# Attention and two dense layers on one core: the first loads regrouped, two transfers at the head of ScalarE's queue, attention jobs due sooner

## The chip, the cores and the metric

The kernel runs on one NeuronCore of one Trainium2 chip. The metric is the device time of one execution in microseconds (us), and the number compared is the median of several runs. The five engines are named here as the profile names them: PE is TensorE, DVE is VectorE, ACT is ScalarE, POOL is GpSimd and SP is SyncE, which here only issues transfers.

## The reference

Causal attention over a window with four sink positions feeds two dense layers. All of it is float32.

```python
batch, n_heads, seq, head_dim = (2, 8, 768, 64)
n_sink, window = (4, 128)
scores = scale * np.matmul(q, k.transpose(0, 1, 3, 2))
keep = is_sink | in_window            # in_window: 0 <= row - column < window
scores = np.where(keep, scores, -1000000000.0)
a = np.exp(scores - max); a = a / (sum(a) + 1e-09)
x = (a @ v) as (1536 tokens, 512)
...
h = x @ w_in                          # layer 0: (512, 2048)
g = np.maximum(h, 0.0) + alpha * np.minimum(h, 0.0)
x = g @ w_out
...
h = x @ w_in; r = np.maximum(h, 0.0)  # layer 1
out = (r * r) @ w_out
```

## The kernel before, in words

**Units of work.** Queries are cut into 12 chunks of 128 rows (six for each batch), and the eight heads into two groups of four, so the attention is 24 *jobs*, counted here from 0; job i is group i % 2 of the chunk that stands i // 2-th in `ORDER`. A job is: scores on TensorE into the bank `s` (L515); a masked minimum on VectorE for each of four heads (L528, into `sp` and `nm`); the exponentials on ScalarE (L532); the normalisation by `rc` (L548 on VectorE or L547 on ScalarE); four transposes on TensorE into `t` (L557); a copy to `pc` on either engine (L240); two selections on GpSimd (L571); the sums with the values into `o` (L590); and two rows that write the attention's output `X` as a high part and a remainder (L240, L247). Jobs 0 to 3 belong to first chunks, have no earlier chunk to look at, and are smaller.

The dense layers split each operand into a high part and a remainder, and make a product of three matmuls. The weights come in 512 KB blocks, a *half* for each of 16 slices of the hidden size and each of the two matrices (L276), stand packed as 64-bit values, and have to be unpacked into `w` by ScalarE and VectorE (L280 to L292: `cs`, `x`, high part, remainder). L308 makes h from `X` and `w`, L318 to L328 make `g` from it, and L340 makes the layer's output from `g` and `w`.

**What sets the order.** Each step is given to a planner (`Plan.add`) with a due time, what it reads and writes, and the engines that could do it at an assumed cost. `Plan.issue` then writes the program: it takes again and again the step with the earliest due time among those that could start soon. The planner's costs (`AFTER`, `MORE`, the start values in L680) set the order and the choice of engine, and nothing else. On the chip each engine runs its own list in order, and waits at each instruction for semaphores.

The due times stand in tables. `JOBS` holds those of the 24 jobs, `RAW_LOADS` those of the first 16 weight halves' transfers, `VALUE_LOADS` those of the first two value tiles. All transfers are issued by SP, but for half of the last store. Queries and keys come in one transfer for each job (L495, L496): 128 KB of queries and 160 KB of keys, the keys into one of four places of a tile for each head group. The queries of jobs 0 to 3 lie in `g7`, a tile that the dense layer uses later.

**Semaphores of transfers.** The framework gives every transfer one of eight completion semaphores in turn, DMAHW0 to DMAHW7, in the order in which the program was written, whatever queue issues it. A transfer whose semaphore was used before waits, on the engine that issues it, until the earlier transfer with that semaphore has landed.

Until the first dense matmul, 34 matmuls of an identity (L699, `WARM`) stand between the attention's, to keep TensorE busy.

Of the kernel before, what the change touches and what calls it, by code (L numbers as in the profile page):

```python
# [18 lines left out]
P = 128  # L19
NS = 32  # L20
KC = P + NS
W3 = 2 * P + NS
# [5 lines left out]
AFTER = {"pe": 197, "act": 150, "dve": 128, "pool": 140, "dma": 950}  # L28
MORE = {"pe": 90, "pool": 40, "dma": 1250}
# [20 lines left out]
SOON = -1000.0  # L50
# [4 lines left out]
ORDER = (0, 6, 1, 7, 2, 3, 4, 5, 8, 9, 10, 11)  # L55
# [115 lines left out]
def attn_moe_moe(ctx, tc, q, k, v, vsink, par, alpha, w1, w2, out):  # L171
    nc = tc.nc
    B, NCH, NG, _, QW = q.shape
# [24 lines left out]
    pari = const.tile([P, 4], I32, name="pari")  # L198
# [53 lines left out]
    class Feed:  # L252
# [9 lines left out]
        def half(self, due, layer, f, slot, a, need):  # L262
            add, new = self.plan.add, self.places.new
            wk = f"w{slot}_{a}"
            w = self.w[layer, f, a] = new(wk)
            q = self.halves
            self.halves += 1
            r, more = self.raws(q)
            early = RAW_LOADS[q:q + 1] if self.early else ()
            rk, ck, xk = f"raw{r}", f"cs{q % 2}", f"x{q % 2}"  # L270
            cs, x = new(ck), new(xk)
# [3 lines left out]
            at = due - PARTS + a  # L275
            add(early[0] if early else due - LOAD + a, more, [rk], ("dma", 1456, lambda: nc.sync.dma_start(out=raw(), in_=src)))  # L276
# [122 lines left out]
    class Short:  # L399
# [65 lines left out]
        def start(self):  # L465
            self.K = [self.con.tile([P, 2, 4 * KC], F32, name=f"K{g}") for g in range(NG)]
            self.v, self.sums, self.early = {}, {}, self.places.new("g7")
            for i in range(B * NCH * NG):
                self.job(i, *divmod(ORDER[i // NG], NCH), i % NG)

        def load(self, due, key, get, src, cost):
            self.add(due, [], [key], ("dma", cost, lambda: nc.sync.dma_start(out=get(), in_=src)))

        def values(self, due, at, key, src):
            t = self.places.new(key)
            self.load(due, key, t, src, 728)
            self.v[at] = t, key

        def job(self, i, b, c, g):
            add, new, K = self.add, self.places.new, self.K[g]  # L480
# [6 lines left out]

            if i < 4:

                qk, qt = ("g", 7, i // 2, i % 2 * 2), lambda: self.early()[:, i // 2, i % 2 * 256:i % 2 * 256 + 256].bitcast(  # L490
                    F32).rearrange("p (a s) -> p a s", a=2)
            else:
                qk, qt = ring("q", 2)
            when = JOB_LOADS[i] if i < 4 else due - 8
            self.load(when, qk, qt, q[b, c, g].rearrange("p (a s) -> p a s", a=2), 364)  # L495
            self.load(when, ("K", g, here), lambda: K[:, :, here * KC:(here + 1) * KC],  # L496
                      k[b, c, g].rearrange("p (a s) -> p a s", a=2), 455)
# [103 lines left out]
    def full_attention():  # L601
        with ExitStack() as ctx:
# [22 lines left out]
            for c in range(NCH):  # L625
# [9 lines left out]
                for b in range(B):  # L635
                    for h in range(2 * 4):
# [3 lines left out]
                        nc.sync.dma_start(out=qt, in_=q[b, c, g].rearrange("p (a s) -> p a s", a=2)[rows, pr % 2])  # L640
                        kt = raw.tile([D, S], F32, tag="kt", name="kt")
                        vv = raw.tile([P, NCH, 2 * D], F32, tag="vv", name="vv")
                        for cc in range(NCH):
                            nc.sync.dma_start(out=kt[:, cc * P:(cc + 1) * P],
                                              in_=k[b, cc, g].rearrange("p (a s) -> p a s", a=2)[rows, pr % 2, 0:P])
                            nc.sync.dma_start(out=vv[:, cc], in_=v[b, cc * P:(cc + 1) * P, pr * 2 * D:(pr + 1) * 2 * D])
# [32 lines left out]
    with tc.manual_schedule():  # L679
        plan = Plan({"pe": 2500, "dve": 4500, "pool": 1500, "act": 1300, "dma": 2900})  # L680
# [9 lines left out]
        nc.sync.dma_start(out=pari, in_=par.bitcast(I32).rearrange("(o n) -> o n", o=1).to_broadcast([P, 4]))  # L690
# [157 lines left out]
```

## Time and profile before

| | us |
|---|---|
| median of three runs | 633.65 (633.64 to 634.35) |
| the profiled execution's own time | 635.78 |
| its span, first to last instruction | 634.1 |
| TensorE busy | 618.5 |
| VectorE busy | 390.3 |
| ScalarE busy | 248.5 |

The span is what the profiler shows; the time has 1.7 us around it. The profiled execution is 2.1 us longer than the median of the runs, so a sum made in the trace is a difference that is then taken off the median. Busy time is the time in which an engine had an instruction in work. It overlaps at instruction boundaries (a row that is 0.69 us long may be followed after 0.61 us), so where durations are added up below, the distance from one start to the next is taken.

### The profile page before, as it was taken

What the parts mean: (1) busy time and instruction counts of PE and PEld (TensorE: products, weight loads), DVE (VectorE), ACT (ScalarE), POOL (GpSimd) and SP (SyncE); (2) the same over time, 40 slices, a digit from 0 to 9 for tenths busy, and PEclk for the clock granted to TensorE, in tenths of its full rate; (3) what the DMA queues carried; (4) which work ended last, traced back from release to release, by engine and by line L of the source; (5) the groups of instructions that cost most, each with busy time, mean ns of one, the idle gap of its engine ahead of it and who ended that gap; (6) DMA issues with size and microseconds to landing.
All of it is one profiled execution on the core that took longest, in us unless ns stands there. A gap on an engine that the chain in (4) does not pass through costs nothing.

```text
span 634.1 us, 9086 instructions
## 1 busy us (share of the span) xinstructions
PE 618.5 (98%) x3448; PEld 512.4 (81%) x3448; DVE 390.3 (62%) x927; ACT 248.5 (39%) x579; POOL 29.1 (5%) x48
## 2 busy tenths in 40 slices
PE   8898999999999999999999999999999999999996
PEld 7787877888888888888888788888888888888885
DVE  6899976678846949363389984233496324444342
ACT  4899865545445625120146661210362211010110
POOL 0013122212000000000000000000000000000000
PEclk9799999999999999999999999999999999999999
DMA  7955223210452434100015540000040000101002
GB/s 243 346 181 175 74 84 95 70 44 11 126 174 70 154 101 163 45 1 1 0 33 188 179 133 1 1 0 1 0 133 1 1 0 1 68 0 37 30 1 71
DMA packets 23428, 48.13 MB, mean 76 GB/s; under 512 B 2512, under 2 KB 11984, under 8 KB 23376
## 3 DMA queue, kind: packets, MB, share of 16 engines
q1 hardware_dynamic: 23232, 47.34, 23.2%
q8 instruction: 29, 0.48, 0.3%
q14 instruction: 23, 0.19, 0.1%
q10 hardware_dynamic: 144, 0.13, 0.1%
HBM read 44.31 MB, written 3.15 MB: 75 GB/s over the span
## 4 chain that ended last, share of the span: by engine, by line
PE 80%; DVE 13%; DMA 3%; issue 1%; SPq 1%; ACT 1%; DVEq 0%; ACTq 0%
PE h L308 35%; PE yb L340 28%; PE h L340 10%; PE o L590 4%; PE s L515 3%; DVE w L247 2%; DVE x L289 2%; DMA al<-alpha 2%; DVE r L320 1%; DVE x L286 1%; PE t L557 1%; DVE g L247 1%; DVE sp L528 1%; DMA raw<-w 1%; DVE X L247 1%
## 5 line engine op out<-in xcount | busy, mean ns | idle before, releaser
L308 PE MATMUL h<-X,w 128*128 128x512 f32 (+1 forms) x1248 | 275.9, 375 | 0.3 <-DVE r L320 0.3
L308 PEld LDWEIGHTS h<-X,w 128*128 128x128 f32 x1248 | 222.3, 189 | 42.8 <-DVE r L320 0.7
L340 PE MATMUL yb<-w,g 128*128 128x512 f32 x576 | 134.5, 389 | 0.0
L340 PEld LDWEIGHTS yb<-w,g 128*128 128x128 f32 x576 | 108.1, 188 | 22.4
L325 DVE TENSOR_TENSOR r<-r 128x512 f32<-128x512 f32 x48 | 33.2, 691 | 122.8 <-ACT r L323 122.8
L323 ACT ACTIVATE r<-h 128x512 f32<-128x512 f32 x48 | 28.7, 598 | 174.5 <-PE h L308 174.4
L340 PE MATMUL h<-g,w 128*128 128x512 f32 x288 | 69.5, 395 | 0.1
L247 DVE TENSOR_TENSOR g<-r,g 128x512 fp32r<-128x512 f32 (+1 forms) x104 | 68.2, 657 | 2.2
L340 PE MATMUL yb<-g,w 128*128 128x512 f32 x288 | 68.7, 391 | 0.2 <-DVE g L247 0.2
L340 PEld LDWEIGHTS yb<-g,w 128*128 128x128 f32 x288 | 53.7, 188 | 12.7 <-DVE g L247 1.6
L340 PEld LDWEIGHTS h<-g,w 128*128 128x128 f32 x288 | 53.2, 189 | 11.4 <-ACT Y L240 0.6
L320 DVE SCALAR_TENSOR_TENSOR r<-r,oma,h 128x512 f32<-128x512 f32 (+1 forms) x56 | 37.2, 666 | 36.3 <-ACT r L318 36.3
L318 ACT ACTIVATE r<-h 128x512 f32<-128x512 f32 (+1 forms) x56 | 29.8, 533 | 59.7 <-PE h L308 59.3
L280 ACT ACTIVATE cs<-raw 128x512 f32<-128x512 f32 x56 | 37.6, 675 | 33.2 <-DVE x L289 24.5
L289 DVE SCALAR_TENSOR_TENSOR x<-cs,x 128x512 uint32<-128x512 uint32 x64 | 43.9, 690 | 1.9 <-ACT x L282 0.2
L247 DVE TENSOR_TENSOR w<-x,w 128x512 fp32r<-128x512 f32 x64 | 43.9, 687 | 1.4 <-ACT w L240 0.4
L532 ACT ACTIVATE sp<-sp,nm 128x160 f32<-128x160 f32 (+1 forms) x96 | 39.8, 417 | 9.8 <-DVE nm L528 9.6
L240 DVE CAST g<-r 128x512 fp32r<-128x512 f32 (+1 forms) x69 | 29.1, 422 | 2.8
L240 DVE CAST w<-x 128x512 fp32r<-128x512 f32 x25 | 10.6, 425 | 28.8 <-PE h L308 18.6
L240 ACT CAST w<-x 128x512 fp32r<-128x512 f32 x39 | 24.0, 616 | 7.1 <-DVE x L289 6.4
L515 PE MATMUL s<-K,q 64*128 64x160 f32 (+1 forms) x320 | 26.2, 305 | 0.1
L286 DVE TENSOR_SCALAR x<-raw 128x512 uint16<-128x512 uint16 x56 | 25.5, 460 | 1.0 <-DMA raw<-w 0.8
(84 smaller groups left out, 460.6 us busy)
## 6 DMA issues: line engine op xcount, KB each, us to landing
raw<-w SPq DMA_DIRECT2D x56, 512.0 KB, 3.8
Y<-w SPq DMA_DIRECT2D x8, 512.0 KB, 7.4
K<-k SPq DMA_DIRECT2D x24, 160.0 KB, 3.1
v<-v SPq DMA_DIRECT2D x12, 256.0 KB, 3.8
out<-Y SPq DMA_DIRECT2D x11, 256.0 KB, 2.0
q<-q SPq DMA_DIRECT2D x20, 128.0 KB, 2.3
g<-q SPq DMA_DIRECT2D x4, 128.0 KB, 3.4
vs<-vsink SPq DMA_DIRECT2D x2, 256.0 KB, 5.3
```

Source lines behind the costliest of these rows:

```text
L240: return lambda: f(**dict(zip(("out", "in_"), get())))
L247: nc.vector.tensor_tensor(out=lo, in0=src, in1=hi.bitcast(F32), op=ALU.subtract)
L280: add(at, [rk], [ck], ("act", 560, lambda: nc.scalar.activation(out=cs(), in_=raw()[:, :, 1].bitcast(F32), func=AF.Abs, scale=2.0 ** -112)))
L286: add(at, [rk], [(xk, 0)], ("dve", dve_ns(512, True), lambda: nc.vector.tensor_scalar(half(U16, 0), raw().bitcast(U16).rearrange("p j (w a ...
L289: add(at, [ck, *two(xk)], two(xk), ("dve", dve_ns(512), lambda: nc.vector.scalar_tensor_tensor(out=x(), in0=cs().bitcast(U32), scalar=3, i ...
L308: nc.tensor.matmul(like(h()[:, 0:n], xs), lhsT=wi()[:, a, kt * P:(kt + 1) * P], rhs=xs, start=kt == 0 and i == 0, stop=kt == KT - 1 and i ...
L318: add(SOON + due, [hk], [rk], ("act", act_ns(n, True), lambda: nc.scalar.activation(out=rs(), in_=hs(), func=AF.Relu, scale=-1.0)))
L320: add(SOON + due, [hk, rk, "oma"], [rk], ("dve", dve_ns(n + 60), lambda: nc.vector.scalar_tensor_tensor(out=rs(), in0=rs(), scalar=oma[:, ...
L325: add(SOON + due, [rk], [rk], ("dve", dve_ns(n), lambda: nc.vector.tensor_tensor(out=rs(), in0=rs(), in1=rs(), op=ALU.mult)))
L340: nc.tensor.matmul(y(), lhsT=lhsT, rhs=rhs, start=first and i == 0, stop=last and i == 2)
L515: nc.tensor.matmul(s()[:, 2 * p + j, x:y], lhsT=qt()[rows, p], rhs=K[rows, p, k0:k0 + y - x], start=True, stop=True)
L532: ("act", act_ns(n) + 190, lambda h=h: nc.scalar.activation(out=sp()[:, h, 0:n], in_=sp()[:, h, 0:n], func=AF.Exp, scale=-1.0, bias=nm()[: ...
```

## The change

Queries and keys of a chunk now lie together in memory for all eight heads. Keys come in one transfer of 320 KB for a chunk, into one of four tiles `K0` to `K3`; the queries of jobs 0 and 1, and of jobs 2 and 3, in one of 256 KB each. Later queries still come one job at a time, now due 10 before the job and not 8. The first chunk's queries and keys are issued ahead of the masks, the keys on ScalarE's queue. ScalarE also issues the keys of the second chunk and the first two weight halves. The due times of jobs 4 to 23 are smaller, and the planner's numbers for transfers differ.

```diff
-AFTER = {"pe": 197, "act": 150, "dve": 128, "pool": 140, "dma": 950}
-MORE = {"pe": 90, "pool": 40, "dma": 1250}
+AFTER = {"pe": 197, "act": 150, "dve": 128, "pool": 140, "dma": 2500}
+MORE = {"pe": 90, "pool": 40, "dma": -300}
...
-JOBS = (0, 0.5, 1, 1.5, 10, 14, 18, 22) + tuple(range(38, 118, 5))
+JOBS = (0, 0, 1, 1.5, 8, 8, 11.5, 15.5) + tuple(range(30, 94, 4))
...
-JOB_LOADS = (-10, -10, -9, -8.5)
-VALUE_LOADS = {0: -8, 6: -6.5}
-RAW_LOADS = tuple(-9.5 + 1.5 * x for x in range(16))
+AHEAD = 10
+VALUE_LOADS = {0: -8.8, 6: -7}
+RAW_LOADS = tuple(-8.9 + 1.5 * x for x in range(16))
...
+            by = nc.scalar if early and q < 2 else nc.sync
+            add(early[0] if early else due - LOAD + a, more, [rk], ("dma", 1456, lambda: by.dma_start(out=raw(), in_=src)))
...
+            self.K = [con.tile([P, NG, 2, KC], F32, name=f"K{i}") for i in range(4)]
+            self.early = self.places.new("g7")
+
+            self.queries(0)
+            self.keys(0, 0, nc.scalar)
...
+        def queries(self, i):
+
+            nc.sync.dma_start(out=self.early()[:, i].bitcast(F32).rearrange("p (g n) -> p g n", g=NG),
+                              in_=q[divmod(ORDER[i], NCH)])
+
+        def keys(self, i, place, by):
+            by.dma_start(out=self.K[place].rearrange("p g a n -> p g (a n)"), in_=k[divmod(ORDER[i], NCH)])
...
+                add(due - AHEAD, [], [("K", here)], ("dma", 862, lambda: i and self.keys(
+                    i // NG, here, nc.scalar if i < 4 else nc.sync)))
...
-        plan = Plan({"pe": 2500, "dve": 4500, "pool": 1500, "act": 1300, "dma": 2900})
+        plan = Plan({"pe": 2500, "dve": 4500, "pool": 1500, "act": 2100, "dma": 800})
```

In the changed kernel the lines are numbered anew: 276 is 277, 308 is 309, 340 is 341, and from 515 on the numbers are 14 higher.

**The head of ScalarE's list.** Before, ScalarE (ACT) loads its table, makes one small exponential, and then runs job 0's exponentials. The names in brackets are the semaphores that a row waits for.

```order
L434 ACT_TABLE_LOAD
L434 ACTIVATE flag_60<-ident_90 1x1 [waits Pool_49]
L532 ACTIVATE sp0_150,sm0_155<-sp0_150,nm0_151 128x128 [waits DVE_49] x4
L280 ACTIVATE cs0_183<-raw0_137 128x512 [waits DMAHW5_49]
L532 ACTIVATE sp1_185,sm1_194<-sp1_185,nm1_186 128x128 [waits DVE_49] x4
```

Now (`g7` is the queries' tile, `raw0` and `raw1` hold weight halves):

```order
L483 DMA K0_89<-k 128x640
L441 ACT_TABLE_LOAD
L441 ACTIVATE flag_60<-ident_97 1x1 [waits Pool_49]
L483 DMA K1_90<-k 128x640 [waits DMAHW3_49]
L277 DMA raw0_131<-w1 128x1024 [waits DMAHW5_49]
L277 DMA raw1_150<-w1 128x1024 [waits DMAHW7_49]
L546 ACTIVATE sp0_154,sm0_158<-sp0_154,nm0_155 128x128 [waits DVE_49] x4
L281 ACTIVATE cs0_185<-raw0_131 128x512 [waits DMAHW5_49]
L546 ACTIVATE sp1_187,sm1_195<-sp1_187,nm1_188 128x128 [waits DVE_49] x4
```

Four transfers stand ahead of job 0's exponentials, and three of them wait. By the turn of the eight semaphores, DMAHW3 is that of the second query transfer, DMAHW5 that of `v1` and DMAHW7 that of the first half that goes into `Y0`.

**The head of SP's list.** Before:

```order
L690 DMA pari_63<-par 128x4
L472 DMA g7_118<-q 128x256
L472 DMA K0_114<-k 128x2x160
L472 DMA g7_118<-q 128x256
L472 DMA K1_115<-k 128x2x160
L276 DMA raw0_137<-w1 128x1024
L472 DMA g7_118<-q 128x256
L472 DMA K0_114<-k 128x2x160
L472 DMA g7_118<-q 128x256 [waits DMAHW0_49]
L472 DMA K1_115<-k 128x2x160 [waits DMAHW1_49]
L472 DMA v0_175<-v 128x512 [waits DMAHW2_49]
L276 DMA raw1_181<-w1 128x1024 [waits DMAHW3_49]
```

Now:

```order
L479 DMA g7_93<-q 128x512
L426 DMA pari_63<-par 128x4
L479 DMA g7_93<-q 128x512
L486 DMA v0_148<-v 128x512
L486 DMA v1_169<-v 128x512
L277 DMA raw2_183<-w1 128x1024
L277 DMA Y0_65<-w1 128x1024
L277 DMA Y0_65<-w1 128x1024 [waits DMAHW0_49]
L486 DMA q0_263<-q 128x256 [waits DMAHW1_49]
L483 DMA K2_91<-k 128x640 [waits DMAHW2_49]
L486 DMA q1_284<-q 128x256 [waits DMAHW4_49]
L277 DMA Y0_65<-w1 128x1024 [waits DMAHW6_49]
```

SP's first seven rows now wait for nothing; `raw0`, `raw1` and two key transfers are gone from here, `raw2` and the blocks for `Y0` stand sooner, and `q0`, `K2`, `q1`, which jobs 4 and 5 need, come before the third block for `Y0`.

**TensorE's list around the first dense matmuls.** Before, from job 3's transposes (`s` is a job's scores, `t` its transposes, `o` its sums, `h` a dense product):

```order
L557 MATMUL t_367<-ident_90,sp1_296 128x128 x4
L590 MATMUL o_379<-pc0_359,v1_211 64x128 x4
L515 MATMUL s_390<-K0_114,q0_372 128x160 x2
...
L590 MATMUL o_406<-pc1_382,v1_211 64x128 x4
L308 MATMUL h0_416<-X_64,w0_0_214 128x256 x6
L308 MATMUL h1_429<-X_64,w1_0_290 128x256 x6
...
L308 MATMUL h0_481<-X_64,w2_0_365 128x256 x9
L515 MATMUL s_497<-K1_115,q1_464 128x160 x2
...
L557 MATMUL t_531<-ident_90,sp0_425 128x128 x4
L308 MATMUL h1_538<-X_64,w3_0_409 128x256 x12
L308 MATMUL h0_570<-X_64,w4_0_470 128x256 x12
L590 MATMUL o_520<-ss0_526,vs0_452 64x128 x2
```

Now, from job 4's scores on:

```order
L529 MATMUL s_333<-K0_89,q0_263 128x160 x2
...
L571 MATMUL t_380<-ident_97,sp1_304 128x128 x4
L604 MATMUL o_392<-pc0_363,v1_169 64x128 x4
L529 MATMUL s_400<-K0_89,q1_284 128x160 x2
...
L604 MATMUL o_421<-pc1_395,v1_169 64x128 x4
L309 MATMUL h0_431<-X_64,w0_0_223 128x256 x6
...
L529 MATMUL s_472<-K1_90,q0_355 128x160 x2
...
L571 MATMUL t_492<-ident_97,sp0_366 128x128 x4
L309 MATMUL h1_446<-X_64,w1_0_302 128x256 x6
L309 MATMUL h0_518<-X_64,w2_0_429 128x256 x12
L571 MATMUL t_552<-ident_97,sp1_443 128x128 x4
L604 MATMUL o_489<-ss0_501,vs0_418 64x128 x2
```

Job 4's scores now stand ahead of job 2's transposes, and job 5's ahead of all dense matmuls (before: behind 33 of them); dense matmuls stand behind what were later jobs' rows. Jobs 4, 5, 6 and 7 finish their sums behind 36, 36, 48 and 72 dense matmuls, where it was 60, 84, 96 and 108; by job 10's sums both lists have 204, and from job 12 on the counts differ by 3 at most.

## Rows read from the trace of the kernel before

**Rows 1.** The page: busy us of each engine, then tenths in 40 slices.
```profile
PE 618.5 (98%) x3448; PEld 512.4 (81%) x3448; DVE 390.3 (62%) x927; ACT 248.5 (39%) x579; POOL 29.1 (5%) x48
...
DVE  6899976678846949363389984233496324444342
ACT  4899865545445625120146661210362211010110
```

**Rows 2.** By stretch: length, busy us (x instructions), granted clock, DMA share, GB/s.
```profile
0.00:12.00 12.00, 9.28 (x59) 8.26 (x59) 7.42 (x40) 5.35 (x19) 1.14 (x8) 1.00 0.75 221
12.00:28.00 16.00, 14.10 (x109) 11.44 (x108) 12.97 (x46) 12.50 (x37) 0.00 (x0) 0.82 0.94 336
28.00:88.00 60.00, 55.18 (x544) 48.76 (x545) 59.45 (x195) 53.24 (x159) 11.40 (x14) 0.99 0.50 153
88.00:165.00 77.00, 76.88 (x704) 62.02 (x703) 53.63 (x195) 38.23 (x136) 16.57 (x26) 1.00 0.17 49
```

**Rows 3.** What TensorE waited for from 27 to 130 us: total, times, longest.
```profile
PE o L563 <- DVE X L247: 1.3, 1, 1.3
PE t L557 <- DVE sp L548: 1.3, 1, 1.3
PE o L563 <- DVE mask L542: 1.0, 2, 0.6
```

**Rows 4.** Timeline of ScalarE and VectorE at the start; idle before in brackets.
```profile
7.19 0.40 ACT L532 ACTIVATE sp<-sp,nm 128x128 f32<-128x128 f32 x1 [4.89 <-DVE nm L528]
...
8.37 0.47 DVE L284 TENSOR_SCALAR x<-raw 128x512 uint16<-128x512 uint16 x1 [0.59 <-DMA raw<-w]
...
13.65 0.69 ACT L280 ACTIVATE cs<-raw 128x512 f32<-128x512 f32 x1 [2.26 <-DMA raw<-w]
```

**Rows 5.** Transfers, first 40 us: GB/s by us; KB, us to landing.
```profile
GB/s 0 0 53 254 197 256 290 353 326 261 299 369 283 231 330 410 414 434 406 391 374 411 407 383 131 213 213 342 335 308 406 376 394 123 49 197 321 187 327 293
...
raw<-w SPq DMA_DIRECT2D x6, 512.0 KB, 7.1
K<-k SPq DMA_DIRECT2D x10, 160.0 KB, 4.5
v<-v SPq DMA_DIRECT2D x4, 256.0 KB, 5.2
```

**Rows 6.** Transfers issued from 1.0 to 1.5 us: KB each, us to landing.
```profile
g<-q SPq DMA_DIRECT2D x1, 128.0 KB, 2.6
```

**Rows 7.** Timeline of VectorE from 28.5 to 69 us, rows that follow each other.
```profile
28.50 0.42 DVE L247 TENSOR_TENSOR X<-o,X 128x256 fp32r<-128x256 f32 x1
28.84 0.31 DVE L528 CUSTOM_DVE_ANT_0 sp<-s,mask 128x160 f32<-128x160 f32 x1
...
29.56 0.69 DVE L247 TENSOR_TENSOR w<-x,w 128x512 fp32r<-128x512 f32 x1
30.17 0.68 DVE L289 SCALAR_TENSOR_TENSOR x<-cs,x 128x512 uint32<-128x512 uint32 x1
30.77 0.16 DVE L537 TENSOR_SCALAR rc<-sm 128x4 f32<-128x4 f32 x1
30.84 0.46 DVE L284 TENSOR_SCALAR x<-Y 128x512 uint16<-128x512 uint16 x1
31.19 0.47 DVE L320 SCALAR_TENSOR_TENSOR r<-r,oma,h 128x256 f32<-128x256 f32 x1
...
68.58 0.69 DVE L548 TENSOR_TENSOR sp<-sp,rc 128x512 f32<-128x512 f32 x1
```

**Rows 8.** Timeline of TensorE at four places.
```profile
24.53 2.29 PE L515 MATMUL s<-K,q 64*128 64x160 f32 x16
...
27.80 3.63 PE L308 MATMUL h<-X,w 128*128 128x256 f32 x24
...
64.77 1.26 PE L515 MATMUL s<-K,q 64*128 64x160 f32 x16
...
69.42 0.62 PE L557 MATMUL t<-ident,sp 128*128 128x128 f32 x4
```

More of the change, by code (lines that the diff above doesn't have):

```diff
@@ L419, in masks @@
             con = self.con
+            self.K = [con.tile([P, NG, 2, KC], F32, name=f"K{i}") for i in range(4)]
+            self.early = self.places.new("g7")
+            self.queries(0)
+            self.keys(0, 0, nc.scalar)
+            nc.sync.dma_start(out=pari, in_=par.bitcast(I32).rearrange("(o n) -> o n", o=1).to_broadcast([P, 4]))
             self.ident = con.tile([P, P], F32, name="ident")
@@ L465, in start, with load @@
         def start(self):
-            self.K = [self.con.tile([P, 2, 4 * KC], F32, name=f"K{g}") for g in range(NG)]
-            self.v, self.sums, self.early = {}, {}, self.places.new("g7")
+            self.v, self.sums = {}, {}
             for i in range(B * NCH * NG):
                 self.job(i, *divmod(ORDER[i // NG], NCH), i % NG)
-        def load(self, due, key, get, src, cost):
-            self.add(due, [], [key], ("dma", cost, lambda: nc.sync.dma_start(out=get(), in_=src)))
+        def queries(self, i):
[3 more added lines that the diff above has]
+            by.dma_start(out=self.K[place].rearrange("p g a n -> p g (a n)"), in_=k[divmod(ORDER[i], NCH)])
+        def load(self, due, keys, get, src, cost, by=nc.sync):
+            self.add(due, [], keys, ("dma", cost, lambda: by.dma_start(out=get(), in_=src)))
         def values(self, due, at, key, src):
             t = self.places.new(key)
-            self.load(due, key, t, src, 728)
+            self.load(due, [key], t, src, 728)
             self.v[at] = t, key
         def job(self, i, b, c, g):
-            add, new, K = self.add, self.places.new, self.K[g]
+            add, new, K = self.add, self.places.new, self.K
             due, ci = float(JOBS[i]), b * NCH + c
@@ L510, in scores @@
                 for p in range(2):
-                    for x, y, k0 in ((0, KC, before * KC), (KC, W3, here * KC)) if c else ((0, P, here * KC),):
+                    for x, y, at in ((0, KC, before), (KC, W3, here)) if c else ((0, P, here),):
                         for j in range(2):
                             rows = slice(j * D, (j + 1) * D)
-                            nc.tensor.matmul(s()[:, 2 * p + j, x:y], lhsT=qt()[rows, p], rhs=K[rows, p, k0:k0 + y - x],
+                            nc.tensor.matmul(s()[:, 2 * p + j, x:y], lhsT=qt()[rows, p], rhs=K[at][rows, g, p, 0:y - x],
                                              start=True, stop=True)
-            add(SOON + at, [qk, ("K", g, here)] + ([("K", g, before)] if c else []), ["s"], ("pe", 930 if c else 420, scores),
+            add(SOON + at, [qk, ("K", here)] + ([("K", before)] if c else []), ["s"], ("pe", 930 if c else 420, scores),
                 after=self.sums[i - BEHIND] if i >= NFREE else ())
@@ L639, in full_attention @@
                         qt = raw.tile([D, P], F32, tag="qt", name="qt")
-                        nc.sync.dma_start(out=qt, in_=q[b, c, g].rearrange("p (a s) -> p a s", a=2)[rows, pr % 2])
+                        nc.sync.dma_start(out=qt, in_=q[b, c, :, g].rearrange("p (a s) -> p a s", a=2)[rows, pr % 2])
                         kt = raw.tile([D, S], F32, tag="kt", name="kt")
```

23 lines of the change are left out of this document (10 added, 13 removed).

## The prediction

> **What bounds the kernel now.** I read the page first, then the busy time by stretch, then the waits of TensorE, then the timelines. TensorE is busy 98% of the span and VectorE 62% [rows 1], but the slices say that the first 90 us are another kernel than the rest. By stretch [rows 2]: from 88 to 165 us TensorE is busy 76.88 of 77 us; from 28 to 88 us VectorE is busy 59.45 of 60 us and ScalarE 53.24, while TensorE lacks 4.8 us, nearly all of it in waits for rows of VectorE [rows 3]. So time can be won or lost only ahead of about 90 us, and what comes out there is handed down: a TensorE that reaches job 12 a microsecond sooner ends a microsecond sooner. Two quantities decide it. One is how long VectorE stands idle at the start: 12 − 7.42 and 16 − 12.97, so 7.6 us ahead of 28 us [rows 2]. The other is how far the lists let TensorE's work run behind VectorE's.
>
> **How the lists are weighed.** I add up the rows that stand ahead of a point on either engine, from one start to the next: on VectorE 0.60 for a pass over 512 values, 0.35 for the 16-bit unpacking, 0.39 for L320, 0.34 for a remainder of 256, 0.24 for a masked minimum (0.31 less the overlap of 0.08), 0.1 for a reciprocal and the like [rows 7]; on TensorE 1.18 for a job's scores [rows 8], and in the same way 0.44, 1.46 for its transposes and sums, 0.117 and 0.227 for a dense matmul of 256 and 512 columns. Check: the normalisation of job 9 has 59.1 us of VectorE behind it and starts at 68.58, so it ends 10.1 late against pure work; 8.0 of that are idle time by the same count at 28 us, 2.1 rows that took longer than I allow.
>
> **The weak point before is job 9.** Its transposes start at 69.42 [rows 8], right behind their normalisation [rows 7]. On VectorE 59.1 us stand up to there (41 rows of 0.60, 17 of 0.35, 10 of 0.39, 40 minima, 24 of 0.34, the rest small). On TensorE only 51.7 us stand ahead (34 warming matmuls 10.9, eleven jobs' scores 10.7, nine jobs' transposes 4.0 and sums 9.3, 141 dense matmuls 16.5, other 0.5). The difference, 7.4 us, is time that TensorE must lose on top of VectorE's idle time, whatever else is done.
>
> **Jobs sooner (a gain).** In the new list I weigh each job's normalisation in the same way. Jobs 5 to 9 now have at most 1.5 us more VectorE work behind them than TensorE work, and mostly less (before: 2.8, 4.9, 4.2, 0.3, 7.4). The worst is job 12: 77.3 us of VectorE (52 rows of 0.60, 22 of 0.35, 16 of 0.39, 52 minima, 32 of 0.34) against 73.3 of TensorE, so 4.0. The reason is that a job gives TensorE some 3.1 us of work for about 3 us of VectorE, while a weight half takes 2.2 us of VectorE and gives TensorE nothing at once. Gain: 7.4 − 4.0 = 3.4 us. On ScalarE the same comparison falls by about 1 us, so ScalarE does not take its place. Behind job 9 TensorE before loses another 1.5 us in changes between jobs and dense matmuls up to job 12; since the worst point now lies at job 12, these fall inside its wait. At most 1.5 us are won so, at least nothing if TensorE is late by itself; I take 0.7.
>
> **The new head of the queues (a loss).** The second keys, `raw0` and `raw1` go out on ScalarE, but each waits there for the landing of the transfer that had its semaphore: the second queries, `v1`, the first block for `Y0`. Behind them in ScalarE's list are job 0's exponentials, which started at 7.19 [rows 4]; VectorE waits for `raw0`, which was there at 8.37, and for `raw1`, there at 13.65 [rows 4]. When they land now:
> - First bytes. A transfer alone landed after 2.6 us [rows 6]; 128 KB at 277 GB/s are 0.47 of them, so 1.9 to 2.1 us go by first. Transfers now start at about 0.8, so bytes flow from 2.6.
> - `v1`: ahead of it are keys and queries, 320 + 4 × 256 KB with itself, 1376 kB. From 3 to 10 us, where queries, keys and one block of weights moved, the mean was 277 GB/s [rows 5]: 7.5 us. `raw0` goes out then and its bytes flow from 9.4.
> - By 9.4, `raw2` and the second keys, 852 kB, are nearly through at the 400 GB/s that blocks of weights reach (406 to 434 from 15 to 19 us [rows 5]); 100 kB are left. `raw0` and the first `Y0` block make 1048 kB more: both there at 9.4 + 1148/400 = 12.3.
> - `raw1` goes out at 12.3, flows from 14.3 beside the blocks queued on SP, as many bytes again: 16.9.
>
> Job 0's exponentials then start at 12.8, 5.6 later than before. VectorE unpacks `raw0` at 12.3, waits 0.55 and 0.45 for ScalarE, reaches `raw1`'s first row at 15.65 and waits to 16.9. Following ScalarE's list from 12.8 (9.1 us of work up to job 3's exponentials, and 0.85 waiting), I find no longer wait on VectorE up to job 3's `pc` copy, which ends at 28.0 with 17.6 us of rows behind it: 10.4 us idle against 8.0. Loss: 2.4 us. ScalarE itself loses little: before it idled 12 − 5.35 and 16 − 12.50, so 10.2 us, ahead of 28 us [rows 2], and now some 10.9 by the same point.
>
> The ends. If SP's ring goes first, `Y0`'s block is there at 11.0, `raw1` at 15.6, and the loss is 1.1. If all bytes move at 277 GB/s, the landings are 14.4 and 20.1, and it is 5.6. I take the middle one, nearest to the rates of like blocks. The Trainium skill (DMA: Bandwidth & Descriptors, Queues, rings and completion order) says that an engine of the DMA takes turns between queues a packet at a time; by it the two blocks land together, at 12.3, and by the 11.0 of the other order the total would be 1.3 us less; no run here shows it, since the trace of before has one transfer on ScalarE's queue, at its end. The same page (Issuing engines are not separate DMA queues) holds that a second queue saves issue time alone; by it this part of the change wins nothing, and the sum, which counts the bytes of both queues together, has no gain for it either.
>
> **Costed at nothing.** The table load starts one issue later (0.4 to 0.7 us), and so the identity and job 0's scores (from 5.6 to about 6.2); VectorE's wait for `raw0` hides it, and without that it would be 0.6. Fourteen transfers fewer on SP: SP waits there for buffers, not for its own issues. Keys in one tile for both groups: a reload now waits for both jobs of a chunk, two jobs (some 12 us) ahead of its use, against 3 to 8 us of landing. `K2` lands by about 15, its use is behind 22.
>
> **TensorE's clock.** At 24.53 a job's scores took 2.29 us, at 64.77 1.26 [rows 8]; the granted clock was 0.82 over 12 to 28 us [rows 2], so part of that time was at 1.2 GHz, behind short idle gaps. TensorE will idle more from 11 to 18 us now. If the scores of jobs 4 and 5 and the sums run slow, job 5's come 1.2 us late and VectorE waits that long. I count nothing, since before had such a stretch too, and keep 1.2 for the range.
>
> **Sum.** +2.4 − 3.4 − 0.7 = −1.7 us. Off the median: 633.65 − 1.7 = 632.0. In the profile: span 634.1 to 632.4.
>
> **Rivals.**
> 1. *ScalarE's queue decides: slower.* Everything waits for exponentials behind four transfers. It wins over the cover from a loss of 4.1 us on, that is when `raw0` and the `Y0` block land after about 14.0. At 277 GB/s throughout: +5.6 − 3.4 = +2.2, 635.9. For it: GB/s fell to 231 at 13 us [rows 5]. Against it: blocks of weights moved at over 400.
> 2. *The two cancel.* The loss is 3 to 4, by a slow clock (+1.2) or somewhat later landings, and nothing comes of the 0.7: 633.65, within 0.2% (1.3 us, about what a measurement of this kernel can tell from no change).
> 3. *Early landing and full cover.* Loss 1.1, and all 1.5 won: −3.8, 629.9. For it: queries and keys now come in rows of 2 KB and more.
> 4. *The change does not do what it says.* Nothing gets ahead of all else, since ScalarE's transfers wait: that is in my sum. That jobs do not move is excluded by the counts of dense matmuls.
>
> **How the numbers follow.** My forecast, −0.7 to −2.7 us (631.0 to 633.0), has 0.46, rival 3 0.15, rival 2 0.14, rival 1 0.25. The part of the forecast that lies within 1.3 us of before counts as no change (0.12 of the 0.46), so faster 0.34 + 0.15 = 0.49, same 0.12 + 0.14 = 0.26, slower 0.25. The range of 629.9 to 635.9 takes in both ends.
>
> **What would show it.** Right: job 0's first exponential between 11.5 and 14; VectorE idle about 10 us ahead of 28 us; first dense matmul at 28 to 31 us; TensorE's waits for VectorE from 28 to 90 us down by a third or more, with the granted clock 1.00 from about 31. Wrong: exponentials after 14.5; VectorE idle over 2 us between 28 and 60 us (a tighter chain of jobs that I didn't see); or a wait of TensorE for keys, values or queries there.

## The result, and the profile after

The kernel after takes 638.56 us (median of 4 runs, 638.03 to 639.05) against 633.89 for the kernel before: 1.0073 times as long (95% interval 1.0055 to 1.009), 4.7 us more. The prediction was 632.0, its range 629.9 to 635.9: wrong in sign, and 2.7 us outside. Rival 1 (ScalarE's queue decides) named the place and the sign, and put 635.9 on it.

The page of the kernel after, as in [rows 1]: VectorE's and ScalarE's first slice (16 us) fall from six and four tenths to three and two.

```profile
PE 618.6 (97%) x3448; PEld 512.7 (81%) x3448; DVE 388.8 (61%) x924; ACT 253.0 (40%) x591; POOL 29.1 (5%) x48
...
DVE  3999997667755949554289993333396424434342
ACT  2888985556654725321045671111262201010110
```

By stretch, as in [rows 2]:

```profile
0.00:12.00 12.00, 8.54 (x48) 7.50 (x48) 3.93 (x24) 2.57 (x8) 1.14 (x8) 1.00 0.80 281
12.00:28.00 16.00, 11.51 (x95) 10.00 (x96) 11.74 (x52) 10.83 (x40) 0.00 (x0) 0.89 0.50 188
28.00:88.00 60.00, 55.93 (x547) 48.94 (x547) 58.94 (x189) 53.25 (x159) 11.39 (x14) 0.97 0.47 158
88.00:165.00 77.00, 76.75 (x698) 62.13 (x695) 55.85 (x203) 46.13 (x156) 15.90 (x25) 1.00 0.21 66
```

VectorE is idle for 8.07 + 4.26 = 12.3 us ahead of 28 us; forecast were 10.4. From 28 us on nothing got worse in busy time: VectorE 58.94 of 60, TensorE 55.93. So by busy time the loss lies ahead of 28 us; behind it the granted clock of 0.97, where the control below has 1.00, leaves a part open. The waits of VectorE up to 34 us (total, times, longest) say for what:

```profile
DVE x L285 <- DMA raw<-w: 5.8, 1, 5.8
DVE parf L450 <- DMA pari<-par: 3.7, 1, 3.7
```

ScalarE's list at the start, with its transfers (ACTq), to be read against [rows 4]:

```profile
0.81 0.41 ACTq L483 DMA_DIRECT2D K<-k  x1
...
6.66 0.34 ACTq L483 DMA_DIRECT2D K<-k  x1
7.97 2.90 ACTq L277 DMA_DIRECT2D raw<-w  x2
10.92 0.40 ACT L546 ACTIVATE sp<-sp,nm 128x128 f32<-128x128 f32 x1 [8.17 <-DMA Y<-w]
...
14.82 0.68 ACT L281 ACTIVATE cs<-raw 128x512 f32<-128x512 f32 x1 [2.26 <-DMA raw<-w]
```

The second keys go out at 6.66 us, `raw0` at 7.97, `raw1` at about 10.5, each behind the landing that it waits for, and job 0's first exponential stands behind them all at 10.92 (before: 7.19). `raw0` is there at 14.82 (before: 8.37). The row at 10.92 names its releaser as a block for `Y0`, which ScalarE never reads: the wait is `raw1`'s, one place ahead in the list, for the transfer that had its semaphore.

What SP had issued by then, besides the queries, values and bounds that stand first in its list:

```profile
3.14 0.43 SPq L277 DMA_DIRECT2D raw<-w  x1
3.61 1.15 SPq L277 DMA_DIRECT2D Y<-w  x2
4.81 0.65 SPq L486 DMA_DIRECT2D q<-q  x1
5.90 0.33 SPq L483 DMA_DIRECT2D K<-k  x1
7.31 0.33 SPq L486 DMA_DIRECT2D q<-q  x1
```

And GB/s in slices of half a microsecond from 0 to 20 us:

```profile
GB/s 0 0 0 41 144 391 412 218 74 63 132 324 406 397 434 410 426 410 426 410 409 424 405 393 426 380 411 391 410 393 408 393 393 403 396 398 394 391 241 31
```

From 6 to 19 us the transfers move at some 400 GB/s. So `raw0` is not late for want of bandwidth, but because it comes so far behind. All transfers issued up to it make 4288 KB, or 4.39 MB; by 14.5 us the slices add up to 4.38 MB. The trace also tells the queues apart: q1 is SP's, q10 ScalarE's (packets, MB, share of the engines' time). From 4 to 10 us, from 10 to 12 us, and from 12 to 14.5 us:

```profile
q1 hardware_dynamic: 825, 1.96, 93.2%
...
q1 hardware_dynamic: 188, 0.47, 59.2%
q10 hardware_dynamic: 140, 0.34, 43.2%
...
q10 hardware_dynamic: 176, 0.62, 62.8%
q1 hardware_dynamic: 233, 0.39, 41.9%
```

From 4 to 10 us ScalarE's queue moved nothing, though the second keys went out on it at 6.66. Their first packet starts at 10.17 us and their last ends at 12.2; `raw0`, behind them in the same queue, moves from 11.8 to 14.2. Meanwhile SP's first block for `Y0`, issued at 3.61, had landed at 10.5.

One thing about the base. The profiled execution of before that the prediction worked from was 2.1 us longer than the median of its runs, so the two traces differ by 2.2 us where the times differ by 4.7. A second profile of the kernel before (the control, below) has the median's time. Of the 17 runs of the kernel before beside the control, the ten shortest (up to 633.95 us) have a mean granted clock of 0.997 to 0.999 and the seven others (from 634.21) 0.991 to 0.996; the first profile, at 0.994, is of the second kind.

### The profile page after: what moved, and what is told of

It is laid out like the page before. It is cut to its first block, busy times and chain, and to the rows that moved or that the text cites. A ratio compares the mean times of both kernels' runs of the same rounds, so it can differ in the third digit from the quotient of the medians.

```text
span 636.3 us, 9094 instructions
## 1 busy us (share of the span) xinstructions
PE 618.6 (97%) x3448; PEld 512.7 (81%) x3448; DVE 388.8 (61%) x924; ACT 253.0 (40%) x591; POOL 29.1 (5%) x48
## 4 chain that ended last, share of the span: by engine, by line
PE 88%; DVE 9%; DMA 2%; ACT 0%; issue 0%; SPq 0%; DVEq 0%
PE h L309 38%; PE yb L341 31%; PE h L341 10%; PE o L604 4%; PE s L529 3%; PE t L571 1%; DMA raw<-w 1%; DVE x L290 1%; DVE sp L542 1%; DVE w L247 1%; DVE r L321 1%; DVE x L287 1%; PE h L712 1%; DMA v<-v 1%; DVE g L247 1%; DVE s L536 1%
## 5 line engine op out<-in xcount | busy, mean ns | idle before, releaser
L546 ACT ACTIVATE sp<-sp,nm 128x160 f32<-128x160 f32 (+1 forms) x96 | 39.8, 417 | 11.8 <-DMA Y<-w 8.2
```

The lines of the kernel that those rows point to most:

```text
L546: ("act", act_ns(n) + 190, lambda h=h: nc.scalar.activation(out=sp()[:, h, 0:n], in_=sp()[:, h, 0:n], func=AF.Exp, scale=-1.0, bias=nm()[: ...
```

## The experiments

Theory A: the loss is made at the head of the queues. Its rival, theory B: the new order of the jobs costs the time. Behind the first four runs A splits into A1 (the waits in ScalarE's list cost) and A2 (two queues at once cost).

Times are medians beside runs of the kernel before on the same chip (633.5 to 634.0); a ratio is to those.

**The kernel before once more (`control`).** No edit.

> The kernel before once more, for a second profile of it. The shown profile of before is 2.1 us longer than the median of its timed runs, and its clock falls to 0.6 at 20 to 30 us. Both theories: 633.4 to 634.4 us in time. If that profile was an odd one, this span is near 632.0, and some 2 us of the distance to the kernel after were hidden by it; if a profile costs 2 us, the span is again near 634.

633.83 us, ratio 0.9996 (0.9984 to 1.0009); the profiled execution has a span of 632.0. By stretch:

```profile
0.00:12.00 12.00, 9.28 (x57) 8.19 (x58) 7.28 (x39) 5.36 (x19) 1.14 (x8) 1.00 0.74 217
12.00:28.00 16.00, 14.12 (x127) 11.75 (x126) 14.56 (x56) 13.44 (x41) 0.00 (x0) 1.00 0.97 343
28.00:88.00 60.00, 54.77 (x541) 48.08 (x540) 59.55 (x196) 54.14 (x165) 11.85 (x15) 1.00 0.47 152
```

The clock is 1.00 where [rows 2] have 0.82, and VectorE is idle for 4.72 + 1.44 = 6.2 us ahead of 28 us, not 7.6. Against this start the kernel after loses 12.33 − 6.16 = 6.2 us of VectorE.

**All transfers on SP (`head_all_on_sp`).** The list of TensorE and VectorE is that of after, row for row.

```diff
-            by = nc.scalar if early and q < 2 else nc.sync
+            by = nc.sync
-            self.keys(0, 0, nc.scalar)
+            self.keys(0, 0, nc.sync)
-                    i // NG, here, nc.scalar if i < 4 else nc.sync)))
+                    i // NG, here, nc.sync)))
```

> The kernel after with its four transfers on ScalarE's queue (first and second keys, raw0, raw1) issued by SP instead, in the same place of the program; the order on TensorE and VectorE stays as it is. Theory A (the loss is made at the head: ScalarE's transfers wait for the landing of transfers that had their semaphores, raw0 lands at 14.8 us and job 0's exponentials wait behind it): raw0 lands by about 8.5, first exponential near 8, VectorE idle ahead of 28 us falls from 12.3 to 7.5 to 8.5 us, time 633.5 to 635.0 us. Theory B (the new order of jobs costs the time, the head little): 637.5 to 639.0.

631.26 us, ratio 0.9954 (0.9937 to 0.9972): 7.3 us less than after, and 2.5 less than before. By stretch, and the first exponential and the first row that needs `raw0`:

```profile
0.00:12.00 12.00, 8.78 (x54) 7.78 (x56) 5.98 (x36) 4.74 (x16) 1.14 (x8) 1.00 0.80 271
12.00:28.00 16.00, 15.74 (x151) 13.25 (x148) 15.65 (x67) 14.04 (x49) 0.00 (x0) 1.00 0.88 316
28.00:88.00 60.00, 55.73 (x559) 48.80 (x560) 59.85 (x186) 52.99 (x156) 12.52 (x16) 1.00 0.42 143
...
8.49 0.40 ACT L546 ACTIVATE sp<-sp,nm 128x128 f32<-128x128 f32 x1 [6.18 <-DVE nm L542]
...
9.96 0.46 DVE L285 TENSOR_SCALAR x<-raw 128x512 uint16<-128x512 uint16 x1 [0.87 <-DMA raw<-w]
```

Theory B falls: with the same lists on the engines the time is 7.3 us shorter. It even came out below what theory A expected. VectorE's idle time ahead of 28 us is 6.4, against 6.2 in the control. So the choice of the queue for four transfers costs all of the loss and more, and the rest of the change is worth some −2.5 us.

**The bounds first (`par_first`).** The line that loads `pari` is moved ahead of `self.queries(0)`.

> The kernel after with the 2 KB transfer of the bounds (pari) issued ahead of the first queries, as in the kernel before; nothing else changes. Theory A: pari lands near 3.5 instead of 5.9 us, the first mask is made 1.2 us sooner and job 0's minima start near 6.9; the first exponentials still wait for ScalarE's transfers. If the slow stretch of the transfers at 4 to 5.5 us (63 to 132 GB/s) is pari's, it moves ahead or goes away, and raw0 lands up to 1.5 us sooner: 637.0 to 638.3 us. Theory B: no change, 638.3 to 639.0.

638.91 us, ratio 1.0074 (1.0057 to 1.009): no gain. `pari` landed at 5.3, not at 3.4, while the first keys moved beside it on the other queue, and VectorE waited 6.7 us for `raw0` in place of 5.8. The slow slices moved with it (GB/s by half microseconds from 0 us):

```profile
GB/s 0 0 0 0 31 52 103 129 234 250 400 414 406 410 430 422 426 410 418 393 415 428 388 361 423 388 390 410 370 421 388 434 389 399 376 410 402 385 397 97
```

**Due times alone (`jobs_alone`).** The kernel before with one line changed.

```diff
-JOBS = (0, 0.5, 1, 1.5, 10, 14, 18, 22) + tuple(range(38, 118, 5))
+JOBS = (0, 0, 1, 1.5, 8, 8, 11.5, 15.5) + tuple(range(30, 94, 4))
```

> The kernel before with the new due times of its jobs alone; its transfers and their queue stay, only that a job's loads move with its due time. Theory A, with the forecast's gain for sooner jobs (VectorE's work ahead of TensorE's at the worst job 7.4 to 4.0 us): 629.5 to 631.5 us, TensorE's waits for VectorE between 28 and 90 us down by half. A gain of nothing (the sooner jobs only move the wait): 633.0 to 634.5. Theory B (the new order costs): 635 to 638.

631.0 us, ratio 0.9945 (0.9928 to 0.9962): −2.75. TensorE lacks 2.1 of the 60 us from 28 to 88, where the control lacks 5.2; against that VectorE is, in the profiled execution of 632.78 us, idle for 7.5 us ahead of 28 us, 1.3 more, with the clock at 0.89 from 12 to 28:

```profile
12.00:28.00 16.00, 13.02 (x108) 10.72 (x107) 13.18 (x51) 11.82 (x37) 0.00 (x0) 0.89 0.88 308
28.00:88.00 60.00, 57.93 (x590) 51.18 (x586) 59.97 (x200) 53.48 (x161) 12.00 (x16) 1.00 0.49 157
```

**What on ScalarE's queue costs: three kernels.** First `scalar_no_wait`: keys and `raw0` on ScalarE, but issued back to back ahead of its table load, when no semaphore has to be used again; `raw1` goes out on SP.

```diff
-            self.queries(0)
-            self.keys(0, 0, nc.scalar)
+            self.keys(0, 0, nc.scalar)
+            self.keys(1, 1, nc.scalar)
+            self.raw0 = self.places.new("raw0")
+            nc.scalar.dma_start(out=self.raw0(), in_=w1[0, :, 0:512].bitcast(U32).rearrange("p (j w) -> p j w", w=2))
+            self.queries(0)
...
-            add(early[0] if early else due - LOAD + a, more, [rk], ("dma", 1456, lambda: by.dma_start(out=raw(), in_=src)))
+            add(early[0] if early else due - LOAD + a, more, [rk], ("dma", 1456, lambda: early and q == 0 or nc.sync.dma_start(out=raw(), in_=src)))
...
```

The lines left out hand `raw0`'s tile to the plan and keep it from loading the second keys again.

> The kernel after with the first and second keys and raw0 issued by ScalarE back to back ahead of its table load, so that none waits for the landing of another transfer; raw1 goes out on SP, behind v0. Order on TensorE and VectorE unchanged. Theory A1 (the waits in ScalarE's list are what costs: transfers that wait for the one that had their semaphore, with the exponentials behind them): raw0 lands near 10 us instead of 14.8, first exponential near 8.5 to 9, VectorE idle ahead of 28 us 7 to 8.5: 631.5 to 633.5 us, near the kernel with all transfers on SP (631.26). Theory A2 (two queues that move at once make the first transfers land late, waits or not): raw0 at 12 to 13, time 634 to 637.

631.54 us, ratio 0.9968 (0.9957 to 0.9979), within 0.3 us of all on SP. ScalarE's list, and VectorE's first row on `raw0`, for which it did not wait:

```profile
0.81 0.89 ACTq L486 DMA_DIRECT2D K<-k  x2
1.73 0.45 ACTq L427 DMA_DIRECT2D raw<-w  x1
2.21 1.28 ACT L444 ACT_TABLE_LOAD   x1 [2.21 <-issue]
...
8.60 0.40 ACT L549 ACTIVATE sp<-sp,nm 128x128 f32<-128x128 f32 x1 [4.89 <-DVE nm L545]
...
9.12 0.45 DVE L285 TENSOR_SCALAR x<-raw 128x512 uint16<-128x512 uint16 x1
```

Without waits the second queue is as good as the first (by the ratios the two kernels are 0.9 us apart, and the intervals overlap). What costs is that transfers on it wait. A2 falls. The Trainium skill (DMA: Bandwidth & Descriptors, Issuing engines are not separate DMA queues) says that a second issuing engine saves the issue time alone. The two times agree, 631.54 and 631.26.

Second `keys_on_scalar` (`by = nc.sync`, the keys left on ScalarE):

> The kernel after with raw0 and raw1 issued by SP (4th and 6th there) and the first two chunks' keys left on ScalarE. The second keys still wait there for a landing, at about 5 to 6.7 us, but that is ahead of the first exponential. Theory A1: raw0 lands near 8, first exponential near 8.5, the second keys land near 12, in time for job 2: 631.0 to 633.0. Theory A2: second keys later, job 2's scores behind them: 633 to 635.

632.44 us, ratio 0.9983 (0.9973 to 0.9993), 1.2 more than all on SP: the second keys go out at 5.82 us, and VectorE waits 1.6 us for TensorE's transposes ahead of 34 us, 0 with all on SP.

Third `raws_on_scalar` (the keys on SP, `raw0` and `raw1` left on ScalarE):

> The kernel after with the keys issued by SP and raw0 and raw1 left on ScalarE. Two transfers still wait there, now for earlier ones (pari, landed at about 6, and the second keys or queries at 7 to 8), and job 0's exponentials stand behind them. Theory A1: raw0 goes out near 6 and lands near 12.5, exponentials start near 8.5 to 9, VectorE idle ahead of 28 us 9.5 to 10.5: 634 to 637 us. That the keys were the cost: 631 to 632.5.

637.28 us, ratio 1.0057 (1.0043 to 1.007), a little above what was expected. Here the exponentials are not late, and `raw0` is, at 14.05:

```profile
5.64 2.16 ACTq L277 DMA_DIRECT2D raw<-w  x2
8.17 0.40 ACT L546 ACTIVATE sp<-sp,nm 128x128 f32<-128x128 f32 x1 [5.86 <-DVE nm L542]
...
14.05 0.47 DVE L285 TENSOR_SCALAR x<-raw 128x512 uint16<-128x512 uint16 x1 [5.28 <-DMA raw<-w]
```

So `raw0` and `raw1` on ScalarE cost 6.0 of the 7.3 us; the exponentials, which stand behind the transfers in the kernel after, and the keys together make the other 1.3, by subtraction. A transfer that waits in ScalarE's list also starts late once it is out: here `raw0` goes out at 5.64, with nothing ahead of it in its queue, and its first packet starts at 9.86, 4.2 us later. In `keys_on_scalar` and in the kernel after the second keys take 3.5 us for this (5.82 to 9.34, 6.66 to 10.17), where the first keys of `scalar_no_wait`, issued at 0.81, start at 1.99. VectorE's list is in order: job 1's minima stand behind the two rows that unpack `raw0`, job 2's scores behind these minima. In the kernel after TensorE waited 4.8 us there:

```profile
PE s L529 <- DVE nm L542: 4.8, 1, 4.8
```

**All on SP with the bounds first (`all_on_sp_par_first`).** The two edits together.

> The kernel after with all transfers on SP and the bounds (pari) issued first, as in the kernel before: the second step put right beside the first. pari alone landed at 3.4 us, and with queries and keys ahead of it at 5.9, for which VectorE waited 3.8 us. Theory A: job 0's exponentials from 8.5 to about 7.3, raw0 perhaps 0.4 later; 0.3 to 1.2 us less than the 631.26 of all on SP: 630.0 to 631.0. If raw0 decides there instead, no change: 631.0 to 631.8.

632.14 us, ratio 0.9976 (0.9966 to 0.9986): no gain. The exponentials did start at 7.07, but VectorE then waited 2.2 us for `raw0`, which was there at 9.82. From 1.5 to 3.5 us next to nothing moved (1, 30, 5 and 1 GB/s in four slices), while the 2 KB of `pari` went to 128 partitions.

**The bounds on ScalarE's queue (`par_on_scalar`).** All on SP, but `pari` issued first by ScalarE.

> All transfers on SP but the 2 KB of the bounds (pari), which ScalarE issues first of all, with nothing ahead of it and nothing behind it to wait. If the two queues serve it at once with the first queries and keys: pari lands at 3.5 to 5, job 0's exponentials from 8.5 to 7.2 to 8.0, VectorE idle ahead of 28 us some 0.5 us less than the 6.4 of all on SP: 630.5 to 631.2 us. If its small packets only slow the first queries and keys by as much: 631.2 to 632.2.

630.87 us, ratio 0.9952 (0.9935 to 0.997); idle ahead of 28 us 5.9 in place of 6.4, as expected. `pari` landed at 5.16, `raw0` was there at 8.70. The gain of 0.4 us is no more than the two intervals leave open.

**TensorE kept busy (`tensor_filled`).** Is the clock part of the loss? In the kernel after, by stretch:

```profile
13.00:15.00 2.00, 0.00 (x0) 0.00 (x0) 0.17 (x1) 0.18 (x1) 0.00 (x0) 1.00 1.04 401
15.00:17.00 2.00, 0.51 (x4) 0.52 (x6) 2.00 (x12) 1.67 (x7) 0.00 (x0) 0.80 1.03 399
17.00:19.00 2.00, 2.00 (x14) 1.77 (x11) 1.92 (x8) 1.65 (x7) 0.00 (x0) 0.50 1.04 395
...
43.00:46.00 3.00, 2.40 (x21) 2.21 (x23) 3.00 (x14) 2.36 (x7) 0.00 (x0) 0.58 0.74 264
```

0.50 is all of a stretch at 1.2 GHz; TensorE had done nothing from 13 to 15 us. The edit: one warming matmul becomes eighteen.

```diff
-            plan.add(FIRST + i, [], [f"h{i % 2}"], ("pe", 213, lambda h=places.new(f"h{i % 2}"): nc.tensor.matmul(
-                h()[:, 0:P], lhsT=att.ident, rhs=att.ident, start=True, stop=True)))
+            plan.add(FIRST + i, [], [f"h{i % 2}"], ("pe", 213, lambda h=places.new(f"h{i % 2}"), n=18 if i == 15 else 1: [nc.tensor.matmul(
+                h()[:, 0:P], lhsT=att.ident, rhs=att.ident, start=True, stop=True) for _ in range(n)]))
```

> The kernel after with 17 more warming matmuls of the identity where TensorE stood idle for 4.8 us ahead of job 2's scores (11.7 to 16.5 us); nothing else changes, and these matmuls end before the scores can start. In the kernel after the granted clock fell to 0.80, 0.50 and 0.85 from 15 to 21 us, behind that idle time, and to 0.58 at 43 to 46 us. If the clock has a share in the loss: clock 1.00 from 15 to 21 us, and 0.3 to 1.2 us less than 638.56: 637.3 to 638.2. If it has none: 638.3 to 639.0.

637.71 us, ratio 1.0057 (1.0041 to 1.0073): in the range expected for a share of the clock, but overlapping the interval of after. In the profiled execution, of 639.47 us, the low clock moved and did not go:

```profile
13.00:15.00 2.00, 2.00 (x18) 1.81 (x17) 0.00 (x0) 0.00 (x0) 0.00 (x0) 1.00 1.03 392
15.00:17.00 2.00, 0.33 (x5) 0.33 (x6) 1.99 (x12) 1.65 (x6) 0.00 (x0) 1.00 1.03 406
17.00:19.00 2.00, 2.00 (x16) 1.72 (x12) 0.72 (x3) 1.52 (x6) 0.00 (x0) 0.66 1.03 392
...
21.00:23.00 2.00, 2.00 (x11) 2.00 (x11) 2.00 (x10) 2.00 (x10) 0.00 (x0) 0.50 0.02 4
```

The five other executions had a mean granted clock of 0.995 to 0.998 and took 637.0 to 638.2 us (median 637.5); the four of the kernel after had 0.990 to 0.993 and took 638.0 to 639.1. With all on SP it is 0.997. So the clock's share of the 7.3 us is about 1 us, an estimate from these medians; with the overlap of the intervals it is likely and not shown.

**Old due times in both (`merge_alone`, `after_old_dues`).** The `JOBS` line of before, once with all transfers on SP, once with the kernel after as it is; the planner's new numbers stay.

> The kernel with all transfers on SP (631.26 us) with the old due times of its jobs: what is left of the change is the larger transfers in their new order. If sooner jobs win what they won in the kernel before (633.75 to 631.0): 634.0. If they win the forecast's 3.4 to 4.1 us where the start is undisturbed: 634.7 to 635.4. If the larger transfers bring a gain of their own: under 633.3.

> The kernel after with the old due times of its jobs; ScalarE's four transfers stay as they are. Theory A (the head costs some 7 us and the sooner jobs win 2.7 in either kernel): 641.3, by the forecast's gain 642 to 642.7. If the late start had swallowed the gain of the sooner jobs: 638.3 to 639.

629.72 us, ratio 0.9929 (0.9913 to 0.9946), and 637.22, ratio 1.005 (1.0033 to 1.0067). What was expected of the due times fell in both; only the last clause of the first, a gain of the larger transfers (under 633.3), agrees. With the larger transfers the sooner due times, which won 2.75 us in the kernel before, cost 1.5 and 1.3 us (in each pair the intervals just overlap, but both pairs say the same). The start does not explain it; with all on SP and old due times VectorE is idle for 5.94 us ahead of 28 us:

```profile
0.00:12.00 12.00, 7.92 (x56) 7.00 (x56) 6.06 (x36) 4.86 (x17) 1.14 (x8) 1.00 0.81 274
12.00:28.00 16.00, 14.71 (x145) 12.65 (x142) 16.00 (x64) 15.46 (x51) 0.00 (x0) 1.00 0.90 341
28.00:88.00 60.00, 56.04 (x537) 49.43 (x536) 58.60 (x191) 54.18 (x158) 12.08 (x16) 1.00 0.43 138
```

Weighed as in the prediction, the worst job of this list (job 12) has 2.4 us more of VectorE's work behind it than of TensorE's: less than the 4.0 of the kernel after. So with the other parts in place the sooner due times raise this figure. (In the kernel before, weighed in the same way, they lower 7.4 to about 6.0, at job 11, and won 2.75.) Which of the other parts lowers it?

**The planner's numbers alone (`planner_numbers_alone`)**, in the kernel before:

```diff
-AFTER = {"pe": 197, "act": 150, "dve": 128, "pool": 140, "dma": 950}
-MORE = {"pe": 90, "pool": 40, "dma": 1250}
+AFTER = {"pe": 197, "act": 150, "dve": 128, "pool": 140, "dma": 2500}
+MORE = {"pe": 90, "pool": 40, "dma": -300}
-        plan = Plan({"pe": 2500, "dve": 4500, "pool": 1500, "act": 1300, "dma": 2900})
+        plan = Plan({"pe": 2500, "dve": 4500, "pool": 1500, "act": 2100, "dma": 800})
```

> The kernel before with the planner's new numbers for transfers alone (2500 and -300 for a transfer's result and its wait, 2100 and 800 where ScalarE's and the transfers' lists begin); transfers and due times as before. By the weighing of the lists the worst job's lag is 8.3 us at job 11 instead of 7.4 at job 9: 634 to 635.5 us. If the new numbers were the source of the gain: 630 to 632.

634.5 us, ratio 1.0019 (1.0008 to 1.003): slower by 1 us, as the weighing had it. In the profiled execution VectorE is also idle for 7.1 us ahead of 28 us, where the control has 6.2, so the list need not be the cause.

**The larger transfers alone (`loads_alone`)**: all on SP, due times and planner's numbers of before.

> The larger transfers in their new order, all on SP, with the old due times and the planner's old numbers for transfers. By the weighing the worst lag is 4.3 us at job 12, VectorE's idle time ahead of 28 us some 6 to 6.5 us as in the kernel before (6.2): 630.0 to 631.5 us. If the gain needs the planner's new numbers: 633 to 634.5.

632.64 us, ratio 0.9987 (0.9976 to 0.9998): −0.9, where −2.1 to −3.5 were expected; idle ahead of 28 us 6.2, as expected. So +1.0 and −0.9 apart, and −3.9 together (629.72): neither part alone brings the gain; the planner makes another list of both. The weighing puts the four lists of 8.3, 7.4, 4.3 and 2.4 in the right order (`jobs_alone`, with 6.0, falls out of it), but not at the right price: 7.4 to 4.3 would be 3.1 us, and 0.9 were won; 7.4 to 2.4 with both would be 5.0, and 3.9 were won.

**The fastest, and the bounds on ScalarE (`best_par_on_scalar`).**

> The larger transfers with old due times and the planner's new numbers, all on SP (629.72 us), but the bounds issued first on ScalarE's queue. VectorE waits some 0.7 us less for the bounds, as it did with the new due times (631.26 to 630.87): 629.0 to 629.6 us. If raw0 lands later by as much: 629.6 to 630.2.

629.96 us, ratio 0.9944 (0.9927 to 0.9962), the same as 629.72: VectorE's idle time fell from 5.9 to 5.2 us, but the time did not follow. So the larger transfers, all on SP, with the planner's new numbers and the old due times beat both kernels: 0.7% below before, 1.4% below after.

## Why the prediction was wrong

**The failed step is the new head of the queues, put at a loss of 2.4 us.** It costs 6.2 us of VectorE's time (12.3 against the control's 6.2), and 7.3 us of the whole when undone. Of the 3.8 us that the forecast lacks, 1.9 are idle time that it did not see (12.3 against 10.4), the others are in its base. Three things were off.

- *The landing.* "`raw0` and the first `Y0` block make 1048 kB more: both there at 12.3." The wait was right: `raw0` waited for `v1` and went out at 7.97 (forecast 7.5). The overlap of the two queues was wrong. The forecast had the second keys nearly through by 9.4, and `raw0`'s bytes flowing from there on beside the first `Y0` block. In the trace that block landed at 10.5; the second keys start at 10.2 and `raw0` behind them at 11.8, and turns between the two queues show only from 10 us on. `raw0`'s lateness lies in this start: its bytes then took 2.5 us, where 2.9 were forecast. In bytes: SP had issued by then, beyond the list of the prediction, the second `Y0` block, two of the later jobs' queries and the third keys: 512 + 2 × 128 + 320 = 1088 KB, 1.11 MB, at 406 GB/s 2.7 us. 12.3 + 2.7 = 15.0; `raw0` was there at 14.8. And they did move first: of the 3.21 MB that SP had issued ahead of `raw0`, 3.10 had moved by 14.5 us (0.28 up to 4 us, and the q1 rows above). The prediction followed what ScalarE's transfers wait for, and did not follow SP's list to the same instant. No run takes these bytes away, and why ScalarE's queue starts so late is open.
- *The base.* VectorE's 8.0 us of idle time before came from one profiled execution. The control has 6.2.
- *The clock*, counted as nothing and 1.2 us for the range. It fell to 1.2 GHz behind TensorE's 4.8 us of idle time and again in part of 43 to 49 us, where the forecast had 1.00 from 31. By `tensor_filled` it costs about 1 us, which is likely and not shown.

**Jobs sooner, a gain of 3.4 us, and 0.7 behind it.** Forecast were 4.1 us, half as much again as came, and the reason given does not hold in this kernel. With all on SP the rest of the change wins 2.5 us, at 0.2 us more idle time at the start, so 2.7 by the lists, if idle time counts in full. The fall from 7.4 to 4.0 us was read off the whole new list and put down to the due times. Alone, they do win (−2.75); with the larger transfers and the planner's numbers in place, they cost 1.3 to 1.5. The reading behind it was loose too: [rows 3] hold 3.6 of the 4.8 us that TensorE lacks from 28 to 88 us, not nearly all.

**The sum, mended:** +6.2 at the start, −2.7 by the lists, is +3.5; measured +4.7. The 1.2 us left over are near the 1 us estimated for the clock; whatever is not named here shares them.

**What was to show it.** First exponential 11.5 to 14: at 10.92, and not what decided. Idle time about 10: 12.3. First dense matmul 28 to 31: at 31.61. TensorE's waits for VectorE from 28 us on down by a third: 3.6 us in five rows from 28 to 90 us, against 3.9 in four in the trace of before and 4.4 in the control's, so not by a third. Of the signs against it, neither idle time of VectorE from 28 to 60 us nor waits of TensorE for keys or queries came. Rival 1 was to win from a loss of 4.1 us, with `raw0` after about 14.0: it came at 14.8. What rival 1 took for its cause (exponentials behind four transfers) is worth at most 1.3 of the 7.3 us; `raw0` and `raw1` on that queue are worth 6.0 with the exponentials on time.

**Costed at nothing.** Shared keys, fewer transfers (14 in all, but 18 on SP), the third keys: no wait for them shows. The bounds, which the change moves behind queries, were not priced at all: VectorE waits 3.7 us for them, 1.2 in the control. Putting them back first gained nothing in either place: VectorE then waits for `raw0`, which came no sooner, or hardly (15.10 against 14.83 us; with all on SP 9.82 against 9.96).

## What to carry to other kernels

A transfer put on another engine's queue to go ahead has to be followed to its issue: if its completion semaphore is in use, it waits in that engine's list, with that engine's work behind it, while the first queue goes on filling. Count every byte that both queues have issued by that instant. That count fitted `raw0` here and in `raws_on_scalar` (3.80 MB issued, 3.77 moved by 13.5 us, `raw0` there at 14.05); for a transfer that goes out early it is too small, since later ones move beside it (`scalar_no_wait`: 1.70 MB issued up to `raw0`, over 2.0 moved when it landed at 8.8). Issue such transfers where nothing has to be waited for, or leave them on the one queue in the order of need. When a planner makes the order, its parts cannot be priced one at a time: weigh the finished list, as a hint and not as a price, and take a base from more than one profiled execution.

## What the runs showed of the hardware

- While a transfer of 2 KB to 128 partitions (16 bytes each) moved, little else did for some 1.5 to 2.5 us: 63 to 132 GB/s from 4 to 5.5 us in the kernel after, 1 to 30 GB/s from 1.5 to 3.5 us with all on SP and this transfer first, and 58 to 144 GB/s from 2 to 4.5 us over both queues when ScalarE issued it (`par_on_scalar`), where the transfers otherwise reach some 400. The slow stretch moved with it; no run leaves it out.
- A second issuing queue, used without waits, was neither faster nor slower (631.54 against 631.26 us).
- A transfer issued on ScalarE's queue while SP's was full moved its first packet 3.5 to 4.2 us after its issue (three kernels); one issued at the start took 1.2 to 1.5 us.
- The same list of TensorE had a stretch at 1.2 GHz in one kernel and none in the other: 0.58 from 43 to 46 us in the kernel after, behind 1.5 us of idle time, and 1.00 throughout from 28 to 88 us with all on SP, behind the same 1.5 us. What sets them apart was not found.
